# Waits for GpSimd behind VectorE's turn at the shared port, and a two-instruction conversion step planned as two

## The chip, the cores and the metric

One core of a Trainium2 chip runs the whole program. The metric is the device time of one execution in microseconds (us), from the first to the last instruction with the launch around it; the times given are medians of repeated runs. The engines are named as in the profile: PE is TensorE, DVE is VectorE, ACT is ScalarE, POOL is GpSimd, SP is SyncE.

## What is computed

Three stages follow each other, all in float32 (cut from the reference):

```python
# 1: attention with random features, 4 x 8 heads, 576 tokens, 64 wide, 128 features
h = x @ omega.T - (x * x).sum(-1, keepdims=True) / 2;  phi = exp(h - h.max(-1)) / sqrt(m)
num = q_p @ (k_p.T @ v);  x = num / (q_p @ k_p.sum(2) + 1e-6)
# 2: Fourier mixing over tokens and channels, layer norm, then 512 -> 2048 -> 512
u = x + real(fft(fft(x, axis=1), axis=2))
x = u + relu(norm(u) @ w_ch1) @ w_ch2
# 3: low-rank mixing over tokens, then a second 512 -> 2048 -> 512
u = x + (x.transpose(0, 2, 1) @ U @ V).transpose(0, 2, 1)
x = u + relu(u @ w_ch1) @ w_ch2
```

## The kernel before, in words

Every product that needs float32 accuracy is made from halves: a high part (written by ACT as a copy) and a low part (the value minus the high part, by DVE or POOL), three matmuls in place of one. 128 partitions by 384 columns is the usual tile of the two big layers. Most of these layers run in a scheme that forms sums and differences of hidden tiles and of weight tiles, so that 7 products serve for 8; these sums are DVE and POOL work as well. The attention and Fourier stages take the first 270 us or so, the two layers the rest, with the low-rank mixing around 620 to 710 us.

The weights of the two big layers come as 64-bit numbers, two 32-bit words each, from which a float32 tile is put together on the chip: 64 tiles of 128 x 512. `conv` (L881) plans one tile as: an SP load, two ACT copies (`a1`), then `a2`, which is two DVE `TENSOR_SCALAR` instructions on the same tile (L874 clamps, L876 shifts and masks; the second reads what the first wrote), then `conv_c` on DVE (L286, both operands in SBUF), then `conv_d` on POOL (L290, an integer add).

The order is not written by hand. `add` (L106) notes each step with the engines that may take it, a planned duration for each, and what it reads and writes. `plan` (L127) then places the steps one by one in a model of the engines, each at the engine that comes free first, those with the least slack first, and picks the engine of a step that may go to two. Steps marked `lock` are those whose DVE or POOL instruction takes the SBUF port that the two engines share: in the model (`held`) such a step on one of them waits until the other's has ended. `emit` (L241) issues the steps in the order of their planned starts. On the chip each engine takes its own instructions in that order, as soon as the data they read and the buffers they write allow it; nothing in the program made before tells POOL to wait for its planned turn at the port.

Of the kernel before, what the change touches and what calls it, by code (L numbers as in the profile page):

```python
# [12 lines left out]
U32 = mybir.dt.uint32  # L13
AF = mybir.ActivationFunctionType
ALU = mybir.AluOpType
# [20 lines left out]
F64_LO = 2.0**-15 * (1 + 0x100000 / 2**23)  # L36
# [55 lines left out]


class Op:
    __slots__ = ("eng", "fn", "lock", "main", "preds", "succs", "lst", "start", "end", "on", "left", "early", "soft", "raw")


class Sched:
    def __init__(self):
        self.on = False  # L100
        self.soft = True
        self.ops = []
        self.writer = {}
        self.readers = {}

    def add(self, eng, fn, r=(), w=(), lock=False, main=False, early=0.0):  # L106
# [5 lines left out]
        o.preds, o.succs, o.raw = set(), [], set()  # L112
        i = len(self.ops)
        for k in r:
            if k in self.writer:
                o.preds.add(self.writer[k])
                o.raw.add(self.writer[k])
            self.readers.setdefault(k, []).append(i)
        for k in w:
            if k in self.writer:  # L120
                o.preds.add(self.writer[k])
                o.raw.add(self.writer[k])
            o.preds.update(self.readers.get(k, ()))
            self.writer[k] = i
            self.readers[k] = []
        o.preds.discard(i)
        self.ops.append(o)  # L127

    def plan(self):
        ops = self.ops  # L130
        for i, o in enumerate(ops):
            for p in o.preds:
                ops[p].succs.append(i)
            o.left, o.on, o.lst = len(o.preds), None, None
# [12 lines left out]
        chain = [i for i, o in enumerate(ops) if o.main]  # L147
        pos, late = 0, 0.0
        nominal = sorted((o.lst, i) for i, o in enumerate(ops) if o.main or o.soft)
        at_ = 0  # L150
        free = dict.fromkeys(ENGS, 0.0)
        cand = {e: [] for e in ENGS}
        held = {"V": 0.0, "G": 0.0}

        def known(i):
            for e in ops[i].eng:
                cand[e].append(i)

        for i, o in enumerate(ops):
            if not o.left:  # L160
                known(i)
        at = {}

        def avail(i, e):
            if (i, e) not in at:
                at[(i, e)] = max([ops[p].end + ((SELF[e] if p in ops[i].raw else 0.0) if ops[p].on == e else LAT[ops[p].on]) for p in ops[i].preds], default=0.0)
# [12 lines left out]
        n, order = len(ops), []  # L179
        while len(order) < n:  # L180
            best = None
            for e in ENGS:
                for i in cand[e]:
                    o = ops[i]
                    if o.main and i != chain[pos]:
                        continue
                    v = max(free[e], avail(i, e))
                    if best is None or v < best[0] - 1e-9:
                        best = (v, e)
            t, e = best  # L190
            now, soon = [], []
            for i in cand[e]:
                o = ops[i]
                if o.main and i != chain[pos]:
                    continue
                v = avail(i, e)
                (now if v <= t + 1e-9 else soon).append((o.lst, i, v))
            l, i, v = min(now)
            o = ops[i]
            if len(o.eng) > 1 and later(i, e, t, late):  # L200
                alt = [x for x in now if len(ops[x[1]].eng) == 1 or not later(x[1], e, t, late)]
                if alt:
                    l, i, v = min(alt)
                    o = ops[i]
                else:
                    free[e] = max([t] + [free[x] for x in o.eng if x != e]) + 0.05
                    continue
            if e == "G" and any(x != i and ops[x].lock and ops[x].lst < l and ops[x].lst + late < t + o.eng["G"] and max([ops[p].end + LAT[ops[p].on] for p in ops[x].preds], default=0.0) < t + 0.3 for x in cand["V"]):
                free["G"] = max(t, free["V"]) + 0.05
                continue  # L210
            d = o.eng[e]
            w = [x for x in soon if x[2] < t + d and x[0] < t + d and x[0] < l]
            if w:
                m = min(x[2] for x in w)
                if l > m + d:
                    free[e] = m
                    continue
            o.start, o.end, o.on = t, t + d, e
            free[e] = t + d
            if o.lock and e in held:  # L220
                held[e] = t + d
            order.append(i)
            if o.main:
                pos += 1
            if o.main or o.soft:
                while at_ < len(nominal) and ops[nominal[at_][1]].on is not None:
# [12 lines left out]
        return order  # L239

    def emit(self):  # L241
        for i in self.plan():
            self.ops[i].fn(self.ops[i].on)


@with_exitstack
def tile_favor_fnet_moe(ctx: ExitStack, tc: tile.TileContext, qT, kT, v1, om, w1a, w2a, uu, vv, w1b, w2b, cs, cd, out):
# [35 lines left out]

    def conv_c(dst, high, s):
        mu = dst.bitcast(U32)
        nc.vector.scalar_tensor_tensor(out=mu, in0=high, scalar=0xC0000000, in1=mu, op0=ALU.bitwise_and, op1=ALU.bitwise_or)  # L286

    def conv_d(dst, high, s, aeng):
        mu = dst.bitcast(U32)
        aeng.tensor_tensor(out=mu, in0=mu, in1=s, op=ALU.add)  # L290

    def conv_b(dst, high, s, aeng=nc.vector):
        conv_c(dst, high, s)
# [58 lines left out]
        return (nxt_[k] - 1) % n  # L352

    def tt(e, o, x, y, op):
        ENG[e].tensor_tensor(out=o, in0=x, in1=y, op=op)  # L355

    def act(o, x, fn=AF.Copy):
        nc.scalar.activation(o, x, fn)  # L358
# [1 line left out]
    def cp(e, o, x):  # L360
        if e == "A":
            act(o, x)
        else:
            ENG[e].tensor_copy(out=o, in_=x)
# [497 lines left out]
    def sk(j):  # L862
        return ("wl", j) if j in (4, 5) else ("w", j - 6 if j in (6, 7) else j % 4 if j // 4 % 2 == 0 else 4 + j % 4)

    def conv(j, ex=()):
# [5 lines left out]

        def a2(e):
            d = box["c"][0]
            nc.vector.tensor_scalar(out=d, in0=d, scalar1=F64_LO, scalar2=F64_HI, op0=ALU.max, op1=ALU.min)  # L874
            mu = d.bitcast(U32)
            nc.vector.tensor_scalar(out=mu, in0=mu, scalar1=3, scalar2=0x3FFFFFF8, op0=ALU.logical_shift_left, op1=ALU.bitwise_and)  # L876
# [642 lines left out]
    def whole():  # L1519
# [109 lines left out]
        lnu_rs(2)  # L1629
        sch.soft = False  # L1630
        loop()
        sch.emit()

    E = mybir.EngineType
    with tc.manual_schedule(engines={E.PE, E.Activation, E.DVE, E.Pool, E.SP}):
# [86 lines left out]
```

## Time and profile before

| | |
|---|---|
| median of 3 runs | 1057.51 us (1056.8 to 1059.26) |
| the profiled execution, its own time | 1059.15 us |
| its span, first to last instruction | 1057.4 us |
| busy: PE, DVE, ACT, POOL | 1022.6, 918.0, 517.1, 434.5 us |
| mean granted clock of PE | 0.981 |

A busy time is the union of an engine's instructions; the rest of the span the engine was idle. What lies around the span (launch, end) is 1059.15 - 1057.4 = 1.75 us.

### The profile page before, as it was taken

The page shows a single profiled execution, that of the slowest core. Times are in us where ns is not written, and L with a number is a line of the kernel's source. Part 1 is how long each engine was busy: PE and PEld are TensorE (multiplying, and loading weights), DVE is VectorE, ACT ScalarE, POOL GpSimd, SP SyncE. Part 2 cuts the span into 40 slices and gives each one's busy share as a digit, 9 for nine tenths or more (in the row PEclk, how much of TensorE's full clock was granted, in tenths as well). Part 3 has the DMA queues.
Part 4 walks back from the last instruction along what each step waited for, and adds up shares of the span by engine and source line. Part 5 has one row for each costly group of instructions (what it writes and reads, how often), then busy time and mean ns, then how long its engine had stood idle before and what let it go on. Part 6 is the DMA issues. An engine that isn't in the chain of part 4 may idle for free.

```text
span 1057.4 us, 17131 instructions
## 1 busy us (share of the span) xinstructions
PE 1022.6 (97%) x6240; PEld 993.6 (94%) x6240; DVE 918.0 (87%) x1886; ACT 517.1 (49%) x1200; POOL 434.5 (41%) x429
## 2 busy tenths in 40 slices
PE   9999998889999999999999998999999999999998
PEld 8988998789899999999999997789999999999998
DVE  5788988697889999989999889989999999987766
ACT  6796767534455433434443456544544443533232
POOL 2275676243323341415442362623554353543211
PEclk9999999789999999999999998989999999999999
DMA  6544320010112200111210102002111111100013
GB/s 189 165 156 130 102 71 1 1 36 26 41 61 80 60 27 10 29 30 51 61 41 20 41 1 81 20 21 61 41 61 40 60 41 61 41 20 1 1 61 119
DMA packets 49091, 57.01 MB, mean 54 GB/s; under 512 B 3120, under 2 KB 42160, under 8 KB 48880
## 3 DMA queue, kind: packets, MB, share of 16 engines
q1 hardware_dynamic: 48720, 53.23, 16.7%
q0 software_dynamic: 288, 2.70, 0.7%
q8 instruction: 49, 0.80, 0.3%
q14 instruction: 34, 0.28, 0.1%
HBM read 51.20 MB, written 4.72 MB: 53 GB/s over the span
## 4 chain that ended last, share of the span: by engine, by line
PE 78%; DVE 14%; ACT 4%; POOL 2%; issue 1%; DMA 0%; SPq 0%; DVEq 0%; ACTq 0%; POOLq 0%
PE ph L964 10%; PE ph L965 10%; PE ph L966 10%; PE p L1225 9%; PE p L1223 9%; PE p L1224 8%; DVE uT L355 3%; PE pj L367 3%; PE kvp L367 3%; PE phu L964 1%; PE phu L965 1%; PE phu L966 1%; PE pn L367 1%; DVE hl L355 1%; PE acc L1000 1%
## 5 line engine op out<-in xcount | busy, mean ns | idle before, releaser
L355 DVE TENSOR_TENSOR uT<-uT,p 128x384 f32<-128x384 f32 x588 | 307.3, 548 | 48.7 <-PE p L1225 47.1
L290 POOL TENSOR_TENSOR w<-w,sc 128x512 uint32<-128x512 uint32 x64 | 95.9, 1502 | 138.8 <-DVE w L286 110.0
L964 PE MATMUL ph<-yh,ah 128*128 128x384 f32 x384 | 130.5, 340 | 0.6 <-ACT yh L358 0.6
L965 PE MATMUL ph<-yl,ah 128*128 128x384 f32 x384 | 130.3, 339 | 0.0
L966 PE MATMUL ph<-yh,al 128*128 128x384 f32 x384 | 130.3, 339 | 0.0
L1225 PE MATMUL p<-hl,bh_s 128*128 128x384 f32 x294 | 100.2, 341 | 3.3 <-DVE hl L355 3.2
L1223 PE MATMUL p<-hh,bh_s 128*128 128x384 f32 x294 | 99.6, 339 | 0.7 <-ACT hh L358 0.7
L1224 PE MATMUL p<-hh,bl_s 128*128 128x384 f32 x294 | 98.7, 336 | 0.0
L964 PE MATMUL ph<-xh,ah 128*128 128x384 f32 x288 | 97.1, 337 | 0.0
L966 PE MATMUL ph<-xh,al 128*128 128x384 f32 x288 | 96.9, 336 | 0.0
L965 PE MATMUL ph<-xl,ah 128*128 128x384 f32 x288 | 96.8, 336 | 0.0
L482 ACT ACTIVATE phi<-pj,mx 128x128 f32<-128x128 f32 x288 | 82.3, 382 | 19.0 <-DVE mx L469 18.8
L355 POOL TENSOR_TENSOR hl<-r,hh 128x384 fp32r<-128x384 f32 x37 | 41.1, 1110 | 108.6 <-ACT hh L358 101.8
L358 ACT ACTIVATE r<-ph 128x384 f32<-128x384 f32 x66 | 32.4, 491 | 102.4 <-PE ph L966 102.3
L358 ACT ACTIVATE hh<-t 128x384 fp32r<-128x384 f32 x72 | 37.9, 527 | 86.4 <-DVE t L949 83.0
L964 PEld LDWEIGHTS ph<-yh,ah 128*128 128x128 f32 x384 | 73.2, 191 | 1.5 <-ACT yh L358 0.8
L965 PEld LDWEIGHTS ph<-yl,ah 128*128 128x128 f32 x384 | 73.0, 190 | 0.7 <-DVE yl L355 0.4
L358 ACT ACTIVATE hh<-f 128x384 fp32r<-128x384 f32 x60 | 31.6, 526 | 85.5 <-DVE f L355 32.2
L966 PEld LDWEIGHTS ph<-yh,al 128*128 128x128 f32 x384 | 73.0, 190 | 0.0
L1223 PE MATMUL p<-hh,bh_a 128*128 128x384 f32 x210 | 71.7, 341 | 0.1
L1225 PE MATMUL p<-hl,bh_a 128*128 128x384 f32 x210 | 71.3, 340 | 0.0
L1224 PE MATMUL p<-hh,bl_a 128*128 128x384 f32 x210 | 71.1, 338 | 0.0
(736 smaller groups left out, 2963.5 us busy)
## 6 DMA issues: line engine op xcount, KB each, us to landing
raw<-in_w1a_dram SPq DMA_DIRECT2D x16, 512.0 KB, 3.8
raw<-in_w2a_dram SPq DMA_DIRECT2D x16, 512.0 KB, 3.7
raw<-in_w2b_dram SPq DMA_DIRECT2D x16, 512.0 KB, 3.6
raw<-in_w1b_dram SPq DMA_DIRECT2D x16, 512.0 KB, 3.8
raw<-in_qT_dram SPq DMA_DIRECT2D x18, 256.0 KB, 3.1
out_dram<-uT SPq DMA_DIRECT2D x24, 192.0 KB, 2.0
raw<-in_kT_dram SPq DMA_DIRECT2D x17, 256.0 KB, 3.2
vt<-in_v_dram SPq DMA_DIRECT2D x16, 260.0 KB, 2.8
```

The lines of the kernel that those rows point to most:

```text
L290: aeng.tensor_tensor(out=mu, in0=mu, in1=s, op=ALU.add)
L355: ENG[e].tensor_tensor(out=o, in0=x, in1=y, op=op)
L358: nc.scalar.activation(o, x, fn)
L367: nc.tensor.matmul(o, w, m, start=start, stop=stop, skip_group_check=True)
L482: nc.scalar.activation(phi_[n][:, h, :], pj_[(n, g)][:, h - 4 * g, :], AF.Exp, bias=mx_[n][:, h : h + 1])
L964: nc.tensor.matmul(ph, wh[:, c], xh[:, r, :], start=(r == 0), stop=False)
L965: nc.tensor.matmul(ph, wh[:, c], xl[:, r, :], start=False, stop=False)
L966: nc.tensor.matmul(ph, wl[:, c], xh[:, r, :], start=False, stop=(r == 3))
L1000: nc.tensor.matmul(a, wh[:, c], hh, start=(f == 0), stop=False)
L1223: nc.tensor.matmul(a, wh[:, cc], hh, start=first, stop=False, skip_group_check=True)
L1224: nc.tensor.matmul(a, wl[:, cc], hh, start=False, stop=False, skip_group_check=True)
L1225: nc.tensor.matmul(a, wh[:, cc], hl, start=False, stop=True, skip_group_check=True)
```

## The change

`conv` plans the two `TENSOR_SCALAR` instructions as two steps, `a2` and `a3`, of 0.4 us each in the planner's numbers, where one step of 0.8 us held both. In `plan`, a POOL step that takes the port is looked at once more when it is placed: `v` is the time at which its own inputs and the POOL step before it would let it start, and `past` the DVE port steps that end after that and no later than its planned start. If there is such a step, apart from one that had simply begun first, POOL's instruction gets a wait (`after`) for the last of them, and its planned start moves behind that DVE step's end by the latency in `LAT`. `emit` hands the wait to the framework as a dependency between the two instructions. Everything that follows is planned with the moved times, so engines and places of other steps change too.

```diff
+        last = {"V": 0.0, "G": 0.0}
+        locked = []
...
             d = o.eng[e]
+            hold = None
+            if e == "G" and o.lock:
+                v = max([last["G"]] + [ops[p].end + (SELF["G"] if ops[p].on == "G" else LAT[ops[p].on]) for p in o.preds])
+                past = [x for x in locked[-40:] if ops[x].end > v and ops[x].end <= t + 1e-6]
+                if past and (len(past) > 1 or ops[past[0]].start > v or t > ops[past[0]].end + 0.1):
+                    hold = past[-1]
...
+            if hold is not None:
+                o.after = hold
+                t = max(t, ops[hold].end + LAT["V"])
             o.start, o.end, o.on = t, t + d, e
...
             if o.lock and e in held:
                 held[e] = t + d
+                if e == "V":
+                    locked.append(i)
+            if e in last:
+                last[e] = t + d
...
-    def emit(self):
+    def emit(self, dep):
         for i in self.plan():
-            self.ops[i].fn(self.ops[i].on)
+            o = self.ops[i]
+            self.ins = None
+            o.fn(o.on)
+            o.ins = self.ins
+            if o.after is not None:
+                dep(o.ins, self.ops[o.after].ins)
...
+    def dep(x, y):
+        tc.add_manual_dep(x, y.name, mybir.DependencyInfo(mybir.DependencyClass.Sync, mybir.DependencyReason.SCHED_ONLY), reason="port")
...
-        add({"V": 0.8}, a2, ex, [sk(j)], lock=True)
+        add({"V": 0.4}, a2, ex, [sk(j)], lock=True)
+        add({"V": 0.4}, a3, ex, [sk(j)], lock=True)
```

The new field `slack` is 0 everywhere. In the changed program 44 POOL instructions carry a wait for a DVE instruction that they did not have, or for a later one than they had. Of 5161 steps 129 change engine: 61 from POOL to DVE, 51 from DVE to POOL, 9 from DVE to ACT, 7 from ACT to DVE, 1 from ACT to POOL. DVE gets 8 instructions more, POOL 9 fewer.

POOL's instructions where the Fourier stage's folds begin, some 62 us into the execution; `z0o` is a sum or difference of folded tokens, `e20o` an intermediate, and the brackets name the engines that an instruction waits for. Before:

```order
34 L355 TENSOR_TENSOR z0o_940<-e20o_880 128x128 [waits Pool_49]
35 L355 TENSOR_TENSOR z0o_940<-e20o_880 128x128
36 L355 TENSOR_TENSOR z0o_980<-eo_1o 128x256 [waits Pool_49]
37 L355 TENSOR_TENSOR z0o_980<-e20o_971 128x128 [waits DVE_49]
38 L355 TENSOR_TENSOR e20e_1022<-eo_1e 128x256 [waits DVE_49,Pool_49]
```

And in the changed program:

```order
34 L376 TENSOR_TENSOR z0o_940<-e20o_880 128x128 [waits DVE_49,Pool_49]
35 L376 TENSOR_TENSOR z0o_940<-e20o_880 128x128
36 L376 TENSOR_TENSOR e20o_971<-eo_1o 128x256 [waits Pool_49]
37 L376 TENSOR_TENSOR z0o_992<-eo_1o 128x256
38 L376 TENSOR_TENSOR zl0o_942<-z0o_940,zh0o_941 128x512 [waits DVE_49,Activation_49]
```

The first `z0o` now waits for a DVE instruction as well, the intermediate `e20o_971` has come over from DVE, and the low part `zl0o_942` has too, with a wait of its own.

DVE's instructions some 80 us into the execution; `x` is a tile of attention output made from `den` and its reciprocal, `abl` a low part that PE waits for, and `w` are weight tiles in conversion. Before:

```order
125 L355 TENSOR_TENSOR abl_0_1220<-ps_0e,abh_0_1219 128x2x146
126 L549 TENSOR_SCALAR den_0_1232<-pn_0_1212 128x4
127 L874 TENSOR_SCALAR w_1205<-w_1205 128x512
128 L876 TENSOR_SCALAR w_1205<-w_1205 128x512
129 L565 RECIPROCAL den_0_1232<-den_0_1232 128x4
130 L355 TENSOR_TENSOR abl_0_1220<-ps_0o,abh_0_1219 128x2x144
131 L549 TENSOR_SCALAR den_1_1256<-pn_1_1234 128x4
132 L554 TENSOR_TENSOR x_1231<-pn_0_1212,den_0_1232 128x256
133 L565 RECIPROCAL den_1_1256<-den_1_1256 128x4
134 L286 SCALAR_TENSOR_TENSOR w_1205<-raw_1142,w_1205 128x512
135 L554 TENSOR_TENSOR x_1231<-pn_1_1234,den_1_1256 128x256
136 L286 SCALAR_TENSOR_TENSOR w_1131<-raw_966,w_1131 128x512
```

And in the changed program, where the same tile of attention output is `x_1209`:

```order
123 L573 TENSOR_SCALAR den_0_1210<-pn_0_1155 128x4
124 L573 TENSOR_SCALAR den_1_1215<-pn_1_1174 128x4
125 L589 RECIPROCAL den_0_1210<-den_0_1210 128x4
126 L589 RECIPROCAL den_1_1215<-den_1_1215 128x4
127 L578 TENSOR_TENSOR x_1209<-pn_0_1155,den_0_1210 128x256
128 L376 TENSOR_TENSOR abl_0_1213<-ps_0e,abh_0_1212 128x2x146
129 L578 TENSOR_TENSOR x_1209<-pn_1_1174,den_1_1215 128x256
130 L898 TENSOR_SCALAR w_1065<-w_1065 128x512
131 L388 COPY qpT_1255<-pt_0_1234 128x512
132 L902 TENSOR_SCALAR w_1065<-w_1065 128x512
133 L898 TENSOR_SCALAR w_1239<-w_1239 128x512
134 L307 SCALAR_TENSOR_TENSOR w_1065<-raw_966,w_1065 128x512
```

Both halves of `x` now stand ahead of the conversions that they stood between, and the two `TENSOR_SCALAR` of a tile (L898 and L902) have another instruction between them. Of the 64 pairs 57 are apart in the changed program.

## Rows read from the trace of the kernel before

**Rows 1.** Windows by stage: length, busy us (instructions) of PE, PEld, DVE, ACT, POOL, clock, DMA.
```profile
0.00:300.00 300.00, 280.48 (x2057) 270.24 (x2057) 239.34 (x541) 187.77 (x525) 142.99 (x152) 0.96 0.28 83
300.00:600.00 300.00, 298.23 (x1706) 296.07 (x1705) 281.56 (x570) 125.01 (x259) 106.67 (x98) 1.00 0.14 42
600.00:710.00 110.00, 102.51 (x544) 89.89 (x544) 98.49 (x189) 61.77 (x125) 51.33 (x51) 0.94 0.10 29
710.00:1057.40 347.40, 341.43 (x1940) 337.37 (x1938) 298.60 (x589) 142.51 (x291) 133.53 (x128) 1.00 0.15 47
```

**Rows 2.** Timeline, first and last stretched DVE instruction: start us, us, engine, line, instruction.
```profile
13.69 0.71 DVE L364 CAST th<-raw 128x512 fp32r<-128x512 f32 x1
...
957.33 0.92 DVE L355 TENSOR_TENSOR w<-w,st 128x256 f32<-128x256 f32 x1
```

**Rows 3.** Lines 876 and 874, tile eo_1e: ns min/median/max, first and last start.
```profile
L876 DVE TENSOR_SCALAR w<-w x64: 426/428/1408, 72.2 to 942.1; 128x512 uint32<-128x512 uint32 x64
L874 DVE TENSOR_SCALAR w<-w x64: 407/420/1521, 71.8 to 941.6; 128x512 f32<-128x512 f32 x64
L355 DVE TENSOR_TENSOR eo_1e<-x,x x3: 674/685/927, 64.1 to 217.4; 128x512 f32<-128x512 f32 x3
```

**Rows 4.** Timeline at 62 to 68 us; brackets: idle before, and who ended it.
```profile
62.73 0.69 DVE L355 TENSOR_TENSOR z0o<-eo_0o 128x256 f32<-128x256 f32 x1
...
64.08 0.93 DVE L355 TENSOR_TENSOR eo_1e<-x,x 128x512 f32<-128x512 f32 x1
64.93 0.41 DVE L355 TENSOR_TENSOR e20o<-eo_1o 128x256 f32<-128x256 f32 x1
...
67.17 0.99 PE L367 MATMUL pn<-kv,qpT 128*128 128x65 f32 x7 [1.13 <-ACT qpT L358]
```

**Rows 5.** Timeline at 78 to 86 us.
```profile
78.09 1.39 DVE L876 TENSOR_SCALAR w<-w 128x512 uint32<-128x512 uint32 x1
...
83.19 1.71 DVE L286 SCALAR_TENSOR_TENSOR w<-raw,w 128x512 uint32<-128x512 uint32 x1
83.23 0.54 PE L702 MATMUL pdp0r<-abh,cdt 128*128 128x290 f32 x2 [0.90 <-ACT qpT L358]
...
84.98 1.27 POOL L290 TENSOR_TENSOR w<-w,sc 128x512 uint32<-128x512 uint32 x1 [0.63 <-DVE w L286]
85.94 0.61 PE L664 MATMUL ps_1e<-cst,zh0e 128*128 128x292 f32 x1 [1.58 <-ACT uT L358]
```

**Rows 6.** Timeline at 263 to 267 us, the third block's layer norm.
```profile
263.92 1.43 POOL L290 TENSOR_TENSOR w<-w,sc 128x512 uint32<-128x512 uint32 x1 [4.41 <-DVE w L286]
264.26 1.52 DVE L355 TENSOR_TENSOR c_2True<-uT,mean 128x384 f32<-128x384 f32 x1
...
265.70 0.55 DVE L355 TENSOR_TENSOR xl<-c_1True,xh 128x384 fp32r<-128x384 f32 x1
266.30 0.45 PE L965 MATMUL phu<-xl,ah 128*128 128x384 f32 x1 [1.23 <-DVE xl L355]
```

**Rows 7.** Timeline at 513 and at 665 us, the big layers.
```profile
513.86 0.44 PE L1225 MATMUL p<-hl,bh_s 128*128 128x384 f32 x1 [0.64 <-DVE hl L355]
...
665.15 1.23 DVE L355 TENSOR_TENSOR hl<-t,hh 128x384 fp32r<-128x384 f32 x1
...
666.44 0.45 PE L1225 MATMUL p<-hl,bh_s 128*128 128x384 f32 x1 [0.66 <-DVE hl L355]
```

**Rows 8.** Timeline at 219 to 228 us: POOL's longest instruction, and a wait of PE.
```profile
219.99 6.66 POOL L290 TENSOR_TENSOR w<-w,sc 128x512 uint32<-128x512 uint32 x1 [3.30 <-ACT zh3o L358]
...
227.15 1.22 PE L849 MATMUL prs<-ident,rc 128*128 128x128 f32 x4 [3.85 <-ACT qs2r L358]
```

**Rows 9.** Windows at 85, 220 and 223 us, columns as in Rows 1.
```profile
85.00:90.00 5.00, 4.05 (x20) 4.06 (x21) 3.57 (x7) 3.87 (x13) 5.00 (x5) 0.66 0.84 245
219.99:226.65 6.66, 3.31 (x21) 2.80 (x19) 6.66 (x19) 0.76 (x2) 6.66 (x2) 0.93 0.26 79
223.00:233.00 10.00, 6.15 (x21) 5.15 (x20) 9.70 (x24) 2.43 (x5) 4.89 (x3) 0.66 0.01 2
```

More of the change, by code (lines that the diff above doesn't have):

```diff
@@ L94 @@
 class Op:
-    __slots__ = ("eng", "fn", "lock", "main", "preds", "succs", "lst", "start", "end", "on", "left", "early", "soft", "raw")
+    __slots__ = ("eng", "fn", "lock", "main", "preds", "succs", "lst", "start", "end", "on", "left", "early", "soft", "raw", "after", "ins", "slack")
 class Sched:
@@ L104, in __init__, with add @@
         self.readers = {}
-    def add(self, eng, fn, r=(), w=(), lock=False, main=False, early=0.0):
+        self.ins = None
+    def add(self, eng, fn, r=(), w=(), lock=False, main=False, early=0.0, slack=0.0):
         if not self.on:
@@ L111, in add @@
         o.eng, o.fn, o.lock, o.main, o.early, o.soft = eng, fn, lock, main, early, self.soft and "P" in eng
-        o.preds, o.succs, o.raw = set(), [], set()
+        o.preds, o.succs, o.raw, o.slack = set(), [], set(), slack
         i = len(self.ops)
@@ L133, in plan @@
                 ops[p].succs.append(i)
-            o.left, o.on, o.lst = len(o.preds), None, None
+            o.left, o.on, o.lst, o.after = len(o.preds), None, None, None
         t = 0.0
@@ L165, in avail @@
             if (i, e) not in at:
-                at[(i, e)] = max([ops[p].end + ((SELF[e] if p in ops[i].raw else 0.0) if ops[p].on == e else LAT[ops[p].on]) for p in ops[i].preds], default=0.0)
+                at[(i, e)] = max([ops[p].end + ((SELF[e] if p in ops[i].raw else 0.0) if ops[p].on == e else LAT[ops[p].on]) for p in ops[i].preds], default=0.0) + ops[i].slack
             v = at[(i, e)]
@@ L239, in plan @@
         return order
-    def emit(self):
+    def emit(self, dep):
         for i in self.plan():
-            self.ops[i].fn(self.ops[i].on)
+            o = self.ops[i]
+            self.ins = None
+            o.fn(o.on)
+            o.ins = self.ins
+            if o.after is not None:
+                dep(o.ins, self.ops[o.after].ins)
 @with_exitstack
@@ L285, in conv_c @@
         mu = dst.bitcast(U32)
-        nc.vector.scalar_tensor_tensor(out=mu, in0=high, scalar=0xC0000000, in1=mu, op0=ALU.bitwise_and, op1=ALU.bitwise_or)
+        sch.ins = nc.vector.scalar_tensor_tensor(out=mu, in0=high, scalar=0xC0000000, in1=mu, op0=ALU.bitwise_and, op1=ALU.bitwise_or).ins
     def conv_d(dst, high, s, aeng):
         mu = dst.bitcast(U32)
-        aeng.tensor_tensor(out=mu, in0=mu, in1=s, op=ALU.add)
+        sch.ins = aeng.tensor_tensor(out=mu, in0=mu, in1=s, op=ALU.add).ins
     def conv_b(dst, high, s, aeng=nc.vector):
@@ L354, in tt @@
     def tt(e, o, x, y, op):
-        ENG[e].tensor_tensor(out=o, in0=x, in1=y, op=op)
+        sch.ins = ENG[e].tensor_tensor(out=o, in0=x, in1=y, op=op).ins
+    def dep(x, y):
+        tc.add_manual_dep(x, y.name, mybir.DependencyInfo(mybir.DependencyClass.Sync, mybir.DependencyReason.SCHED_ONLY), reason="port")
     def act(o, x, fn=AF.Copy):
@@ L363, in cp @@
         else:
-            ENG[e].tensor_copy(out=o, in_=x)
+            sch.ins = ENG[e].tensor_copy(out=o, in_=x).ins
     def mm(o, w, m, start, stop):
@@ L873, in a2, with a3 @@
             d = box["c"][0]
-            nc.vector.tensor_scalar(out=d, in0=d, scalar1=F64_LO, scalar2=F64_HI, op0=ALU.max, op1=ALU.min)
-            mu = d.bitcast(U32)
-            nc.vector.tensor_scalar(out=mu, in0=mu, scalar1=3, scalar2=0x3FFFFFF8, op0=ALU.logical_shift_left, op1=ALU.bitwise_and)
+            sch.ins = nc.vector.tensor_scalar(out=d, in0=d, scalar1=F64_LO, scalar2=F64_HI, op0=ALU.max, op1=ALU.min).ins
+        def a3(e):
+            mu = box["c"][0].bitcast(U32)
+            sch.ins = nc.vector.tensor_scalar(out=mu, in0=mu, scalar1=3, scalar2=0x3FFFFFF8, op0=ALU.logical_shift_left, op1=ALU.bitwise_and).ins
         add({"S": S512}, lambda e: w_load(j), [], [("raw", j % 2)])
         add({"A": 1.1}, a1, [("raw", j % 2)] + ex, [sk(j), ("s", j % 2)])
-        add({"V": 0.8}, a2, ex, [sk(j)], lock=True)
+        add({"V": 0.4}, a2, ex, [sk(j)], lock=True)
+        add({"V": 0.4}, a3, ex, [sk(j)], lock=True)
         add({"V": V512}, lambda e: conv_c(*box["c"]), [("raw", j % 2)] + ex, [sk(j)], lock=True)
@@ L1631, in whole @@
         loop()
-        sch.emit()
+        sch.emit(dep)
     E = mybir.EngineType
```

## The prediction

> **What bounds the kernel now.** I read the windows by stage first [rows 1]. TensorE is the engine with least idle time: 19.5 us (300 - 280.48) in the first 300 us, 1.8 us from 300 to 600, 7.5 us from 600 to 710 and 6.0 us in the last 347, together 34.8 of the 1057.4 us span. A gain can only come out of these 34.8 us, or out of stretches in which TensorE runs at a lower clock. VectorE is second, 281.56 of 300 us from 300 to 600: it has little room there, but TensorE idles only 1.8 us in that stage, so VectorE's lateness is mostly absorbed by work that lies ahead in buffers.
>
> Then I looked in the timeline for VectorE instructions that took longer than others of the same shape. 97 of them are over 0.1 us longer and have a GpSimd instruction running across them; the first is a cast at 13.69 us, the last at 957.33 us [rows 2]. Their excess adds up to 60.3 us. By the order in which the program issues its steps, GpSimd's instruction belongs behind VectorE's in 65 of the 97 (47.0 us): GpSimd's data were there early and it took the port before its turn. The clearest group is L876: the median is 428 ns and the longest 1408, with 13 of the 64 stretched [rows 3]. It reads what L874 wrote just before, and in the pause between the two GpSimd comes in.
>
> 47 us of stretched VectorE work is not 47 us of the span. So the third view is TensorE's idle gaps, each followed back to what was late. The ones over 0.25 us that have a stretched VectorE instruction in their chain are five places:
>
> - 67 us: TensorE idles 1.13 us behind an ACT copy that follows VectorE's work; ahead of it are a difference of folds at 62.73 (0.69 us where the same shape takes 0.41 at 64.93) and an `eo` at 64.08 (0.93 us, median 0.685) [rows 3, 4].
> - 83 and 86 us: gaps of 0.90 and 1.58 us, with L876 at 1.39 and the conversion's L286 at 1.71 us ahead of them [rows 5].
> - 266 us: 1.23 us, behind `c_2True`, 1.52 us under a GpSimd `conv_d` (L290), where the same size takes 0.55 [rows 6].
> - 513.86 us: 0.64 us, behind a `hl` that is late [rows 7].
> - 666 us: 0.66 us, behind a `hl` of 1.23 us [rows 7].
>
> Together the gaps are 6.14 us (1.13 + 0.90 + 1.58 + 1.23 + 0.64 + 0.66). The other idle time comes from elsewhere: the start, ACT and matmul chains, and one gap of 3.85 us at 227 us of the opposite kind [rows 8], below.
>
> **What the change adds and moves.** Instruction work hardly changes: the split of the conversion step adds nothing, since the two instructions existed, and eight more on VectorE for nine fewer on GpSimd are 8 x 0.4 to 0.7 us, 3 to 6 us over 1057, on an engine that idles 139 us (1057.4 - 918.0). The 44 waits cost no instruction of their own; each delays a GpSimd instruction to the end of a VectorE one. What is queued behind it on GpSimd (low parts of weights and of `h`, the next `conv_d`, its two DMA issues) is delayed with it. SP's loads are issued in almost the same order.
>
> The waits are where GpSimd was planned to be late. Of the 65 out-of-turn cases only 15, with 9.4 us of the 47.0, get a wait that directly holds the offender behind the instruction that it stretched. 16 (13.2 us) have the GpSimd instruction planned ahead now or between the two halves of the conversion, 17 (14.4 us) have no wait, and in the rest one of the two has gone to another place or engine. So I don't expect the 47 us to vanish; perhaps half does, and new encounters arise. I therefore price the five places alone, by what stands there in the changed order.
>
> *67 us.* The excess of the fold (0.69 - 0.41 = 0.28) and of `eo` (0.93 - 0.685 = 0.25) is taken away by the wait, and `e20o` (0.41 us) leaves VectorE for GpSimd [rows 3, 4]: 0.94 of the 1.13 us. Bounds: 0 and 1.13. **-0.94**
>
> *83 and 86 us.* Both halves of `x` come ahead of the conversions, so neither a stretched L876 nor L286 stands before them. But a copy of `x` goes from ACT to GpSimd, behind a held `conv_d`, and what waits for it arrives later. Bounds: 0 and 2.48; I take half. **-1.24**
>
> *266 us.* `c_2True` is now several places ahead of the instruction for which the `conv_d` waits, so it can't be stretched: 1.52 - 0.55 = 0.97 of the 1.23 us [rows 6]. **-0.97**
>
> *513 and 666 us.* At 513 half of the 0.64 us; at 666 the excess is 1.23 - 0.55 = 0.68, all of the gap, but another low part now stands before it on GpSimd: 0.4. Bounds: 0 and 1.30 [rows 6, 7]. **-0.7**
>
> *227 us.* Here the late one is GpSimd: its `conv_d` begins at 219.99 and takes 6.66 us, as long as the window in which VectorE is busy for 6.66 us with 19 instructions, one after the other [rows 8, 9]. ACT and TensorE wait for what follows it (3.85 us), and TensorE's clock falls: the mean granted clock is 0.66 from 223 to 233 us. In the changed order the same `conv_d` waits for an instruction near the end of that row and is let go 0.1 to 0.2 us later than it won the port before. The stall stays. **+0.2**
>
> *New encounters.* A block at full size costs what the longest of L874 does over its median, 1.52 - 0.42 = 1.10 us [rows 3]. With 129 steps on other engines I count one that lands where TensorE has nothing ahead; bounds 0 (all covered) and four of them, 4.4 us. **+1.1**
>
> The sum is -0.94 - 1.24 - 0.97 - 0.7 + 0.2 + 1.1 = -2.55 us. The profiled execution would be 1059.15 - 2.55 = 1056.6; it lies 1.64 us above the median of the runs, so the median would be 1057.51 - 2.55 = **1055.0 us**.
>
> **A rule against the change.** The row at 83.19 shows a release: L286 ends at 84.90, GpSimd's `conv_d` starts at 84.98 [rows 5]. The row at 219.99 shows that a waiting GpSimd does not simply get the next turn, as 19 VectorE instructions went by [rows 8, 9].
> The Trainium skill, page "SBUF — State Buffer", section "SBUF: two separate sides", says that the pair is an exclusive lock: whoever starts first holds it for the whole instruction and the other is fully blocked. The stretched rows agree with that. By it a held GpSimd instruction that comes after one VectorE instruction blocks the next one in its place, so the blocks would only move and the sum would be nothing.
>
> **Rivals.**
> *The blocks move on (no change).* A wait that ends with one VectorE instruction lets GpSimd in at the following one, which is then stretched by the same 1.0 us. For it: 33 of the out-of-turn cases get no wait at the place or are planned in front. Against it: at the five places the next instruction is often not one on which TensorE waits. The gains of 3.85 us are cut to about 1 and the new encounters take that: 1057.5 us.
>
> *GpSimd starves behind its wait (slower).* The wait's signal comes some 0.08 us after VectorE's end, and by then VectorE has started the next instruction; in a full row of VectorE work GpSimd then loses again and again, as at 219.99 us. Place: the Fourier stage to 270 us and the stretch from 450 to 600, where 7 more instructions (some 3.9 us) come to VectorE. Price: another stall such as at 227 us, 3.85 us, and the lower clock after it, 10 us at 0.66, which loses up to 3.4 us; less the gains, about +5: 1062 us. It decides as soon as one `conv_d` takes over 4 us and is followed by a TensorE gap.
>
> *The gains are larger.* All of the 6.14 us go, with no new encounter, and the dip of the clock behind the gap at 86 us (0.66 from 85 to 90 us, 1.7 us lost [rows 9]) goes too: 1057.5 - 6.1 - 1.7 = 1049.7 us.
>
> **How the numbers follow.** Chances: small gain as in the sum 0.45 (1052.5 to 1057.5); larger gain 0.15 (1049 to 1052.5); no change 0.18 (1056 to 1059); slower 0.22 (1059.5 to 1064). 0.2% is 2.1 us, about what a measurement of this kernel can tell from no change: below 1055.4 is faster, above 1059.6 slower. The small gain's centre is near the border, so a little over half of it counts as faster: 0.25 + 0.15 = 0.40. Same: 0.20 and most of the no change, 0.15: 0.35. Slower: 0.22, and 0.03 of the no change whose new encounters weigh more. The range of 1050.0 to 1061.5 leaves out the best end of the larger gain and the far part of the slower case; the likeliest case by itself has 1052.5 to 1057.5.
>
> **What would show it.** In the changed kernel's profile, the stretched L876 (there L902) should be fewer than 13 and its mean near the median; the gaps of TensorE at 67 and 266 us should be below 0.3 us; the gaps at 83 and 86 us about half; the `conv_d` near 220 us still above 6 us with its gap behind it. TensorE's idle time should be 32 us or so in place of 34.8. Wrong on the slow side: GpSimd instructions of over 4 us in more places, and TensorE idle behind low parts made by GpSimd. Wrong on the fast side: TensorE idle under 30 us and the dips at 85 or 227 us gone.

## The result, and the profile after

The changed kernel takes 1041.51 us (median, 1040.94 to 1043.4); the kernel before took 1057.95 us beside it. The ratio is 0.9847, 95% interval 0.983 to 0.9865: 16.4 us faster. I had forecast 1055.0 us with a range from 1050.0, so the direction was right and the size far too small. The profiled execution took 1040.94 us, its span is 1039.1 us against 1057.4, 18.3 us less, at a mean granted clock of 0.986 against 0.981. The profiled execution of the kernel before lies 1.2 us above its median and that of the changed kernel 0.6 below, so about 2 of the 18.3 us are the choice of executions.

The windows by stage of the changed kernel, columns as in [rows 1]:

```profile
0.00:300.00 300.00, 282.16 (x2105) 273.61 (x2106) 234.92 (x551) 191.23 (x532) 132.92 (x156) 0.98 0.27 84
300.00:600.00 300.00, 300.00 (x1725) 298.47 (x1724) 274.54 (x576) 130.16 (x270) 108.94 (x103) 1.00 0.14 43
600.00:710.00 110.00, 104.38 (x558) 94.00 (x556) 96.26 (x197) 60.21 (x121) 50.16 (x52) 0.94 0.11 34
710.00:1039.10 329.10, 324.72 (x1858) 323.62 (x1856) 276.77 (x571) 136.53 (x280) 113.98 (x111) 1.00 0.15 46
```

TensorE idles 27.8 us (1039.1 - 1011.3) in place of 34.8. That is only 7.0 of the 18.3 us. The other 11.3 us came out of what the page calls TensorE's busy time, 1022.6 before and 1011.3 now, for the same 6240 matmuls. The row from 300 to 600 shows how to read this: 1725 matmuls in 300 us where 1706 stood before.

The views of the two halves of the conversion in the changed kernel, to be held against [rows 3]:

```profile
L902 DVE TENSOR_SCALAR w<-w x64: 399/421/429, 72.8 to 926.9; 128x512 uint32<-128x512 uint32 x64
L898 DVE TENSOR_SCALAR w<-w x64: 408/422/971, 72.1 to 923.7; 128x512 f32<-128x512 f32 x64
```

No second half is stretched any more (429 ns at most, 1408 before). Read as for the prediction, the stretched VectorE instructions with a GpSimd instruction across them are 43 with 19.1 us, before 97 with 60.3. Out of turn are 5 with 1.1 us, before 65 with 47.0; those that the plan itself puts behind GpSimd rose from 32 (13.3 us) to 38 (18.0 us).

Where the 18.3 us lie shows when the start of each matmul is compared with that of the same matmul before. Differences by stage, in the time of the kernel before (us; the two traces' starts subtracted, the labels are those of the experiments below). Each row is one execution: those of e1, e4 and e7 lie 3.1, 2.4 and 2.3 us above the medians of their kernels, and the first 60 us differ by up to 1.6 us between kernels of the same order (changed kernel, e2, e5, e6).

```
                     0-60  60-120 120-300 300-600 600-720 720-end
changed kernel       -0.1   -4.7    -3.6    -2.9    -3.7    -3.3
e1 waits only        +1.1   +0.1    -1.9    -2.9    -3.6    -2.6
e2 order only        +0.7   -1.3    +2.0    -0.2    -0.5    -2.3
e3 split only         0.0   +1.1     0.0    -0.5    -3.8    -2.4
e5 early waits        0.0   -4.7    -3.5    -0.4    +0.5    -2.3
e6 late waits        +1.5   -1.3    +1.9    -2.9    -1.9    -3.3
e7 split and waits    0.0   -0.1    -2.1    -2.9    -5.5    -3.3
e12 four early       +1.0   -1.8    +4.7    -0.5    -1.7    -2.2
```

9.9 us came from 300 us on, where I had counted 0.7.

### The profile page after: what moved, and what is told of

Same layout as the page of the kernel before. It is cut to its first block, busy times and chain, and to the rows that moved or that the text cites. A ratio compares the mean times of both kernels' runs of the same rounds, so it can differ in the third digit from the quotient of the medians.

```text
span 1039.1 us, 17145 instructions
## 1 busy us (share of the span) xinstructions
PE 1011.3 (97%) x6240; PEld 989.7 (95%) x6240; DVE 882.5 (85%) x1894; ACT 518.1 (50%) x1201; POOL 406.0 (39%) x420
## 3 DMA queue, kind: packets, MB, share of 16 engines
q1 hardware_dynamic: 48720, 53.23, 16.7%
## 4 chain that ended last, share of the span: by engine, by line
PE 91%; DVE 5%; ACT 2%; POOL 1%; issue 1%; DMA 0%; SPq 0%; DVEq 0%; ACTq 0%; POOLq 0%
PE ph L991 11%; PE ph L992 11%; PE ph L993 11%; PE p L1250 10%; PE p L1252 10%; PE p L1251 10%; PE pj L391 4%; PE kvp L391 3%; PE pn L391 2%; PE phu L991 2%; PE phu L992 2%; PE phu L993 1%; PE acc L1027 1%; PE acc L1029 1%; PE acc L1028 1%; PE pt L544 1%
## 5 line engine op out<-in xcount | busy, mean ns | idle before, releaser
L311 POOL TENSOR_TENSOR w<-w,sc 128x512 uint32<-128x512 uint32 x64 | 89.1, 1394 | 175.9 <-DVE w L307 119.3
L382 ACT ACTIVATE hh<-f 128x384 fp32r<-128x384 f32 x60 | 31.6, 527 | 81.4 <-DVE f L376 27.6
```

The source lines that it names most:

```text
L311: sch.ins = aeng.tensor_tensor(out=mu, in0=mu, in1=s, op=ALU.add).ins
```

## The experiments

Theory W: the waits alone keep GpSimd to its turn, and that is the gain. Its rivals: O, the moved order and engines (or the split) make it; M, the blocks move on to the next VectorE instruction; and later a throttle theory, that any wait which thins out GpSimd's starts helps. Medians and ratios stand beside the kernel before on the same chip; "out of turn" is counted as above.

**e1, waits only.** From the changed kernel, the conversion step left as one and no start moved, which gives the order of before:

```diff
-                t = max(t, ops[hold].end + LAT["V"])
...
-        add({"V": 0.4}, a2, ex, [sk(j)], lock=True)
-        add({"V": 0.4}, a3, ex, [sk(j)], lock=True)
+        add({"V": 0.8}, a2, ex, [sk(j)], lock=True)
```

> The order and engines of the kernel before, with 53 waits put on GpSimd instructions by the same rule, no planned start moved and the conversion step left as one. In the trace of before these waits would stand behind 52 of the 65 out-of-turn cases (37.5 of 47.0 us). Theory W (the waits alone keep GpSimd to its turn and that is the gain): stretched VectorE time falls from 60 us to about 23 us; the change took it from 60.3 to 19.1 us for a gain of some 16 us, so 0.4 us per us, and this kernel comes to 1041 to 1046 us. Theory O (the gain is that of the moved order and engines): 1054 to 1060 us. Theory M (a held GpSimd instruction blocks the next VectorE instruction instead): stretched time stays above 45 us and the time stays at 1056 to 1060 us.

1046.41 us, ratio 0.9883 (0.9864 to 0.9902): 11 us of the 16, with order and engines of before. Out of turn 16 with 11.6 us; all stretched time together is some 29 us, more than the 23 expected and far less than M's 45. O alone and M fall. What is left is mostly the second half of the conversion, which no wait guards here. Its view in e1:

```profile
L899 DVE TENSOR_SCALAR w<-w x64: 426/427/1409, 73.0 to 932.4; 128x512 uint32<-128x512 uint32 x64
```

12 of the 64 are still stretched, 13 before.

**e2, order only.** The changed kernel without the dependency:

```diff
-            if o.after is not None:
-                dep(o.ins, self.ops[o.after].ins)
```

> The order, engines and split of the changed kernel, without the 44 waits. Theory W: out-of-turn cases come back, 40 us or more of stretched VectorE time, 1052 to 1060 us. Theory O: 1041 to 1046 us, with few out-of-turn cases. Theory M: as the changed kernel, 1040 to 1044 us, since the waits do nothing.

1058.3 us, ratio 1.0005 (0.9995 to 1.0015), as W had it: out of turn 47 with 30.0 us, all stretched time together some 43 us, and nothing gained. The windows from 300 to 600 us of e1, then of e2:

```profile
300.00:600.00 300.00, 300.00 (x1725) 299.09 (x1723) 274.70 (x575) 127.26 (x263) 104.70 (x100) 1.00 0.14 43
```

```profile
300.00:600.00 300.00, 299.03 (x1707) 296.10 (x1707) 275.07 (x571) 125.07 (x261) 109.05 (x99) 1.00 0.15 43
```

The order of before with waits has the 1725 matmuls of the changed kernel; the order of the changed kernel without waits has 1707, as before.

**e3, split only.** Both edits: the dependency left out as in e2, and the start not moved as in e1.

> The conversion step planned as two instructions and nothing else: no waits, no start moved for them. Theory W: 1053 to 1060 us, out-of-turn cases as before. Theory O in its form that the split lets the planner place work between the two halves: 1043 to 1050 us, with the stretched L876 gone.

1054.14 us, ratio 0.9969 (0.9958 to 0.9981), in W's bounds, but the split has 3.4 us of its own. The second half is stretched once instead of 13 times, since the planner now sets something between the halves and the pause in which GpSimd came in is filled (56 of the 64 pairs have another VectorE instruction between them). Out of turn 41 with 26.3 us.

**e4, no split.** The changed kernel with the conversion step as one (the second edit of e1).

> The waits and the moved planned starts, with the conversion step left as one (62 waits). Theory W: 1041 to 1048 us, and what is left over the changed kernel is the stretched second half of the conversion, 13 cases of some 1 us before, of which the waits don't hold those planned right at its end. Theory O in its split form: 1052 to 1060 us.

1044.28 us, ratio 0.987 (0.9849 to 0.989), as W had it; out of turn 13 with 9.4 us, of which 8 second halves with 7.2 us.

**e5 and e6, waits of one part.** The changed kernel, with this condition, and with its opposite:

```diff
-            if o.after is not None:
+            if o.after is not None and self.ops[o.after].end < 265.0:
```

> The changed kernel with only the 23 of its 44 waits that stand before the planned time 265 us, up to the third block of the Fourier stage; same order. Theory W with the stages independent: the first 300 us as in the changed kernel (8.3 us less than before in the comparison of TensorE's starts), the rest as in the order without waits (3.1 us less): 1046 us (1044 to 1048). If the gain of the early waits is given back later: 1050 us or more.

> The changed kernel with only the 21 later waits; same order. Theory W with the stages independent: the first 300 us as in the order without waits (1.3 us more than before), the rest as in the changed kernel (9.9 us less): 1048 to 1051 us. If the waits of the big layers did nothing, because TensorE has hidden tiles ahead there: 1055 us or more.

1049.41 us, ratio 0.9929 (0.9915 to 0.9942), and 1053.0 us, ratio 0.9962 (0.995 to 0.9975). Both parts gain, and the first 300 us of e5 are those of the changed kernel in the table. But both came out slower than expected, e5 by 1.4 us over its bound and e6 by 2. Against e2, with the ratios, since the runs were on different chips, the two gain 0.76% and 0.43%, some 8.0 and 4.5 us, together 1.19% and 12.6 us; all waits gain 1.58%, 16.7 us. The table puts most of the missing part into 600 to 720 us (e5 and e6 less e2 make -0.9 there, the changed kernel has -3.7), where an order without waits is worth anything from -3.8 (e3) to -0.5 (e2). The granted clock dips to 0.5 there in every one of these runs, for 3.4, 6.8 or 10.2 us at a time; what sets their length stays open.

**e7, split and waits.** The changed kernel without the moved start (the first edit of e1).

> The order of the split alone (e3) with 43 waits by the same rule, no planned start moved. Theory W: the waits are worth 9 us or more on any order: 1041 to 1046 us against 1054 without them. Theory that the planned starts have to move with the waits, or the wait comes in the way of the next VectorE step: 1049 us or more.

1043.38 us, ratio 0.9873 (0.9857 to 0.9889); out of turn 1 with 0.3 us. W holds on a third order: by the ratios some 10 us less than e3, which is this kernel without waits. The moved starts add what the table shows from 60 to 300 us, but by the ratios the changed kernel is only 0.26% below e7, and the intervals overlap.

**e8 and e12, the wrong turn.** The same order, each wait on the VectorE port instruction planned one place, or four places, ahead:

```diff
-                o.after = hold
+                o.after = locked[locked.index(hold) - 1] if locked.index(hold) else None
```

> The changed kernel's order with its 44 waits, each on the VectorE port instruction planned just before the one of the changed kernel. GpSimd then gets loose one turn too soon. Theory W (what counts is whose turn it is): the instruction that was guarded is stretched again, 30 us or more of stretched VectorE time, 1050 to 1058 us. Theory of the throttle (any wait that thins out GpSimd's starts helps, whichever instruction it names): 1041 to 1046 us.

> The changed kernel's order with each wait on the VectorE port instruction four places ahead of the one that the changed kernel names; e8 with one place ahead kept the whole gain. Theory W, with the turn as what counts: GpSimd comes loose some 2 us early, out-of-turn cases come back to 15 us or more, 1048 to 1058 us. Throttle theory (any wait that thins out GpSimd's starts): 1041 to 1044 us.

One place: 1042.27 us, ratio 0.9861 (0.9848 to 0.9874), the whole gain kept, with 14 cases of 6.6 us out of turn. W's forecast for it, 1050 us or more, failed, and the throttle theory's 1041 to 1046 came out. Four places: 1058.55 us, ratio 1.0007 (0.9995 to 1.0019), the whole gain lost, out of turn 48 with 31.6 us. That is W's forecast but for 0.55 us, yet it does not fell the throttle theory, because little of a throttle was left: four places ahead, only 16 of the 44 waits ask for more than the instruction's own data do, and 9 of these 16 instructions start within 0.3 us of the end of the one named. One place ahead these are 41 and 35. So which instruction has to be named is not shown to within one place. What the runs do show is that the gain goes with the time out of turn: 30.0 us in e2, 31.6 in e12 and 26.3 in e3 at 1058.3, 1058.55 and 1054.14 us; 11.6 in e1 and 9.4 in e4 at 1046.41 and 1044.28; 6.6 in e8, 1.1 in the changed kernel and 0.3 in e7 at 1042.27, 1041.51 and 1043.38.

The timelines show why one place ahead is not yet too soon. First the kernel before, then the changed kernel, then e8, around the same `conv_d`:

```profile
507.08 0.69 DVE L286 SCALAR_TENSOR_TENSOR w<-raw,w 128x512 uint32<-128x512 uint32 x1
...
507.75 0.56 DVE L355 TENSOR_TENSOR hl<-f,hh 128x384 fp32r<-128x384 f32 x1
507.85 1.61 POOL L290 TENSOR_TENSOR w<-w,sc 128x512 uint32<-128x512 uint32 x1 [0.69 <-DVE w L286]
508.23 1.51 DVE L355 TENSOR_TENSOR b_s<-w,b_s 128x256 fp32r<-128x256 f32 x1
```

```profile
497.84 0.56 DVE L376 TENSOR_TENSOR hl<-f,hh 128x384 fp32r<-128x384 f32 x1 [0.24 <-ACT hh L382]
498.32 0.42 DVE L898 TENSOR_SCALAR w<-w 128x512 f32<-128x512 f32 x1
498.81 1.29 POOL L311 TENSOR_TENSOR w<-w,sc 128x512 uint32<-128x512 uint32 x1 [1.57 <-DVE w L898]
499.31 0.56 DVE L376 TENSOR_TENSOR uT<-uT,p 128x384 f32<-128x384 f32 x1 [0.57 <-PE p L1252]
499.78 0.55 DVE L976 SCALAR_TENSOR_TENSOR hl<-ph,hh 128x384 fp32r<-128x384 f32 x1
```

```profile
498.27 0.56 DVE L376 TENSOR_TENSOR hl<-f,hh 128x384 fp32r<-128x384 f32 x1 [0.24 <-ACT hh L382]
498.75 0.42 DVE L898 TENSOR_SCALAR w<-w 128x512 f32<-128x512 f32 x1
498.91 1.40 POOL L311 TENSOR_TENSOR w<-w,sc 128x512 uint32<-128x512 uint32 x1 [1.23 <-DVE hl L376]
499.74 0.55 DVE L376 TENSOR_TENSOR uT<-uT,p 128x384 f32<-128x384 f32 x1 [0.57 <-PE p L1252]
```

Before, `conv_d` starts as soon as its data are there, behind L286, and the low part `b_s` behind it takes 1.51 us where 0.42 is usual. In the changed kernel it waits for L898, starts 0.08 us after that has ended (498.32 + 0.42 = 498.74, 498.81), and beside it run instructions that read PSUM (`p`, `ph`), at 0.56 and 0.55 us, unstretched. In e8 it waits for the `hl` one place ahead, but is let go at 498.91, when L898 has run since 498.75: L898 keeps its 0.42 us and `conv_d` takes 1.40 us, 0.11 more. VectorE has here started its next instruction before GpSimd is let go, and so it has for 30 of the 44 held instructions of the changed kernel. A wait that names one place too early can then still come out right: by name the waits of e8 guard 24 of the 47 cases of e2, and 33 fewer are left. 14 did not come out right.

**e9 and e10, the stall at 217 us.** The copy `qs` of the Fourier stage shares a tile with the conversion, the `s` that `conv_d` reads. e9 is the changed kernel with

```diff
-            box["qs"] = cv.tile([128, 512], F32, tag=f"s{si}", name=f"qs{b}{nm}")[:, 0:NEO]
+            box["qs"] = cv.tile([128, NEO], F32, tag="q0", name=f"qs{b}{nm}")
```

and e10 has besides, as e13 below, no moved start late in the plan:

```diff
-                t = max(t, ops[hold].end + LAT["V"])
+                if t < 265.0:
+                    t = max(t, ops[hold].end + LAT["V"])
```

> The changed kernel, same order and waits; the Fourier stage's copy qs has a buffer of its own, where it shared one with the conversion (the tile s that conv_d reads). Theory B (the 4.06 us gap of TensorE at 217 us is the copy qs2r waiting until the late conv_d lets go of the shared buffer): the copy comes some 4 us earlier, TensorE then waits for the reciprocal alone, and 1.5 to 2.5 us go, 1039 to 1041 us, with up to 3.4 us more if the dip of the clock behind it goes. Theory V (VectorE has too much to do there, and the copy's wait is only beside it): the gap stays within 0.5 us of 4.06, 1041 to 1043 us.

> As e9, and beyond the planned time 265 us the waits are given without moving the planned starts (46 waits, 15 steps on other engines, all after 300 us). e7, which moved none, was 1.7 us quicker from 600 to 720 us than the changed kernel. If the order there did that: 1.5 to 2 us under e9, 1036 to 1039 us. If it was the chance of one dip of the clock: as e9.

1044.02 us, ratio 0.9876 (0.9855 to 0.9898), and 1044.5 us, ratio 0.9875 (0.9856 to 0.9894): neither gains on the changed kernel, both lie 2.5 to 3 us above it. Neither theory had this. e14 and e15 show where the loss comes from.

**e13, late starts unmoved.** The second edit of e10 alone.

> The changed kernel with shared buffers as they were; beyond the planned time 265 us the waits are given without moving the planned starts (46 waits, 15 steps on other engines, all after 300 us). If the order made that way is what made e7 quicker from 600 to 720 us: 1039 to 1041 us, with TensorE's matmul step from 720 us on at 174.5 ns as in the changed kernel. If it was the chance of the clock's dips: 1041 to 1043 us.

1040.67 us, ratio 0.9851 (0.9835 to 0.9866). The median lies in the first bounds, but the ratio cannot be told from the changed kernel's 0.9847. No order gain can be claimed from it; e7's 600 to 720 us was likely one shorter dip of the clock, 3.4 us at 692 us where the changed kernel has 6.8.

**e14 and e15, the size of a buffer.** e14 is e9 with `[128, 384]` for `[128, NEO]` (NEO is 290). e15 is the changed kernel with an unused tile in its place:

```diff
     cv = ctx.enter_context(tc.tile_pool(name="cv", bufs=1))
+    pad = cv.tile([128, NEO], F32, tag="q0", name="pad")
+    nc.gpsimd.memset(pad[:, 0:1], 0.0)
```

> As e9, with the own buffer 384 numbers wide (1536 bytes a partition) in place of 290 (1160 bytes). In e9 and e10 alone the matmul step from 720 us on was 175.1 ns, in the twelve other profiles 174.5. Theory A (what lies behind the odd-sized buffer is moved to other addresses, and that costs the step): 174.5 ns again and 1040.5 to 1042 us. Theory Q (the earlier copy itself does it): 175.1 ns and 1043.5 to 1045 us. The gap at 217 us is as in e9 in both, 2.5 us and 0.9 us behind it.

> The changed kernel with an unused buffer of 290 numbers (1160 bytes) in the same place, one element of it set at the start; qs keeps its shared buffer. Theory A: the matmul step from 720 us on is 175.1 ns, and the kernel takes 1043 to 1045 us. Theory Q: 174.5 ns and 1041 to 1043 us.

e14: 1042.29 us, ratio 0.986 (0.9844 to 0.9876). e15: 1045.05 us, ratio 0.9886 (0.9871 to 0.9901). The matmul steps, 174.5 and 175.15 ns, are those of theory A; the times lie 0.3 and 0.05 us above its bounds. The windows from 750 to 1000 us of the changed kernel, e9, e14 and e15, in this order:

```profile
750.00:1000.00 250.00, 250.00 (x1434) 250.00 (x1433) 215.07 (x445) 106.46 (x218) 88.89 (x87) 1.00 0.11 35
```

```profile
750.00:1000.00 250.00, 250.00 (x1430) 250.00 (x1430) 214.55 (x444) 106.55 (x219) 89.41 (x87) 1.00 0.11 35
```

```profile
750.00:1000.00 250.00, 250.00 (x1434) 250.00 (x1433) 215.19 (x445) 106.99 (x219) 90.00 (x87) 1.00 0.11 35
```

```profile
750.00:1000.00 250.00, 250.00 (x1430) 250.00 (x1429) 214.46 (x445) 106.50 (x218) 88.32 (x86) 1.00 0.11 35
```

With the odd buffer, used or not, 1430 matmuls pass in 250 us, without it 1434, and TensorE shows no idle time in any of them. And e14, free of that, shows what the copy's wait was worth. In the changed kernel the copy starts right behind `conv_d`:

```profile
218.79 1.26 POOL L311 TENSOR_TENSOR w<-w,sc 128x512 uint32<-128x512 uint32 x1 [8.79 <-DVE rc L882]
...
220.09 0.41 ACT L382 ACTIVATE qs2r<-pdq2r 128x290 f32<-128x290 f32 x1 [4.47 <-POOL w L311]
```

And in e14:

```profile
216.92 0.41 ACT L382 ACTIVATE qs2r<-pdq2r 128x290 f32<-128x290 f32 x1
...
220.19 1.26 POOL L311 TENSOR_TENSOR w<-w,sc 128x512 uint32<-128x512 uint32 x1 [8.79 <-DVE rc L882]
220.35 1.62 PE L873 MATMUL prs<-ident,rc 128*128 128x128 f32 x6 [2.46 <-DVE rc L882]
...
222.88 1.65 PE L805 MATMUL pmn<-s,ones 128*128 128x384 f32 x2 [0.92 <-DVE pmm2r L376]
```

The copy now comes long before `conv_d`; TensorE waits 2.46 us for VectorE's reciprocal and then 0.92 us for VectorE again, 3.38 us in place of 4.06, and no time is gained that the runs can tell. Theory B's 1.5 to 2.5 us did not go. Theory V is nearer, though 0.68 is a little over its 0.5: what TensorE waits for there is VectorE's row of folds and layer norm.

**e11, a wait in every case.**

```diff
-                if past and (len(past) > 1 or ops[past[0]].start > v or t > ops[past[0]].end + 0.1):
+                if past:
```

> The changed rule without its exception: a GpSimd port step waits for the last VectorE port step that ends between its own readiness and its planned start, in every case (148 waits in place of 44; 142 steps on other engines than in the changed kernel). Theory W: the out-of-turn cases that are left in the changed kernel (5, 1.1 us) are too few to matter, 1040 to 1043 us. If each wait costs something of itself (the signal takes 0.08 to 0.15 us behind the VectorE instruction's end, on an engine that is not the bound): still 1040 to 1044. If the moved plan matters: planned work ends later, 1045 us or more.

1049.2 us, ratio 0.9918 (0.9901 to 0.9934). Nothing is out of turn any more, but the plan of these 148 waits has 24.1 us of VectorE time behind GpSimd, against 18.0, and the layer around 600 to 720 us costs 1.6 us more than before where the changed kernel saves 3.7. So keeping every turn is not enough. Which part of the loss the waits make and which the 142 steps on other engines, this run does not separate. No version beats the changed kernel by what the runs can tell.

## Why the prediction was wrong

**The five places.** The step of the sum that failed is "I therefore price the five places alone". By the starts of the matmuls behind the gaps they came to -0.58 us (67 us), -2.5 (83 and 86), -0.96 (266), -0.77 (513) and -0.82 (666), together -5.6, where I had -3.85; a new gap at 74 us took 0.6 back, where I had 1.1. Only at 513 and 666 us does that pass a bound, 1.59 for 1.30. The other 13 or so of the 18.3 us lie outside the five places, where I had no gain: 9.9 us came from 300 us on, and only 1.6 of them at 513 and 666. The prediction's own sign of being wrong on the fast side, TensorE idle under 30 us and the dip at 85 us gone, came true.

Gaps of TensorE in the changed kernel, in its timeline:

```profile
66.45 1.11 PE L391 MATMUL pn<-kv,qpT 128*128 128x65 f32 x8 [0.55 <-ACT qpT L382]
...
74.23 1.08 PE L391 MATMUL pn<-kv,qpT 128*128 128x65 f32 x8 [0.95 <-DVE x L578]
...
220.56 0.79 PE L873 MATMUL prs<-ident,rc 128*128 128x128 f32 x2 [4.06 <-ACT qs2r L382]
...
258.01 0.45 PE L992 MATMUL phu<-xl,ah 128*128 128x384 f32 x1 [0.27 <-DVE xl L376]
```

At 67 us [rows 4] 1.13 became 0.55, -0.58 where I had -0.94. At 266 us [rows 6] 1.23 became 0.27: -0.96, where I had -0.97. At 513 us I had -0.3, at 666 us -0.4; no gap is left at either. From 60 to 120 us the starts give -4.7, where I had -0.94 and -1.24: the gaps at 83 and 86 us [rows 5] are gone but for 0.44, and the dip of the clock behind them [rows 9] with them. That dip was in my rival of larger gains; it belonged in the sum.

**What the list left out.** It said that no other gap over 0.25 us has a stretched VectorE instruction in its chain. But the kernel before has this one, with the first half of a conversion stretched from 0.42 to 0.98 us ahead of it:

```profile
644.59 0.98 DVE L874 TENSOR_SCALAR w<-w 128x512 f32<-128x512 f32 x1
...
646.46 0.97 PE L1454 MATMUL pu<-vh,mxl 96*128 96x288 f32 x2 [1.33 <-DVE uT L355]
```

The start behind it moved by -1.15 us. Three more gaps, of 0.68 us at 386.47, 0.70 at 669.15 and 0.69 at 827.13, end a wait for VectorE or for what follows it and are gone as well, -0.84, -0.86 and -0.85 us; how far back VectorE's lateness there goes was not traced.

**What the idle time hides.** "A gain can only come out of these 34.8 us" or the lower clock was wrong too, and so was the sentence that VectorE's lateness from 300 us on "is mostly absorbed". TensorE's idle time is less than its loss. Rows of the kernel before, TensorE at 385 us:

```profile
385.28 0.34 PE L965 MATMUL ph<-xl,ah 128*128 128x384 f32 x1
385.45 0.34 PE L966 MATMUL ph<-xh,al 128*128 128x384 f32 x1
386.47 0.44 PE L1223 MATMUL p<-hh,bh_s 128*128 128x384 f32 x1 [0.68 <-ACT hh L358]
```

Each matmul is shown as 0.34 us, but the next begins 0.17 us after it. From 385.45 to 386.47 are 1.02 us, a loss of 0.85 where the page has 0.68 of idle; a halt of under 0.17 us shows none. Counted by starts, less the usual step of each shape (0.173 us for 128x384), TensorE lost 74.9 us before and loses 56.6 now. The difference of 18.3 us must be the span's, since the matmuls are the same; the two sums depend on the step taken. From 300 to 600 us it lost 6.3 (idle 1.8), now 3.3; with the median step, 0.174 us, 4.6 and 1.6.

So the 18.3 us are 7.0 of idle time, some 5 of the clock and some 6 that show as neither. The clock's part: 1057.4 x (1 - 0.981) = 20.1 us of full speed were withheld before, 1039.1 x (1 - 0.986) = 14.5 now. The dip behind 86 us is gone, one of 3.4 us at 185 us too, and the one of 10.2 us behind 192 us is now 6.8. The last is in part chance: in e14 and e15, with the same order, it is 10.2 us again.

**What the waits reach.** I counted 15 cases (9.4 us) as directly held and took half of 47 us to vanish, with new encounters at +1.1. 60 of the 65 went, and 45.9 of the 47.0 us. The moved order alone took less than half of that: in e2 47 cases with 30.0 us are left. Of these 47 the 44 waits hold 35 by a wait on the GpSimd instruction itself, and 7 more because GpSimd takes its instructions in order, so that a wait holds everything behind it as well. That leaves 5, as found. I had compared the waits with the cases in the old order, and so missed those that the new order makes and the waits then hold. In e1, the old order, the waits stand behind 52 of the 65 cases. And the new plan doesn't set GpSimd anew where it collides: of the 44 held instructions 43 start 0.08 to 0.26 us after the end of the named one, and only 7 have a stretched VectorE instruction beside them.

**The 227 us stall.** The size was right, +0.2 predicted and 4.06 for 3.85 us [rows 8], though a new gap of 1.65 us, a wait for VectorE, stands ahead of it at 214.49 us. The cause was half right. `conv_d` was late and held the copy through the shared tile, but most of TensorE's wait stays without it (e14). And I expected it above 6 us again: 5.4 of its 6.66 us were waiting, as the same instruction now takes 1.26 us (218.79 in the changed kernel, above) and the copy still follows right behind it. GpSimd's time beyond the usual of each shape fell from 31.8 to 13.8 us in all; no run separates what that is worth.

**The rivals.** *The blocks move on* fell with e1 and the seven of 44. In the changed kernel 660 VectorE instructions that read PSUM run beside GpSimd for over 0.1 us, and none is stretched; of 111 with two inputs from SBUF 33 are, and of 57 with one input, from SBUF, 10, all of them `TENSOR_SCALAR` or casts. So the block doesn't move on where the plan has a reader of PSUM next, as at 499.31 and 499.78, and I had overlooked that. The rule of the Trainium skill, page "SBUF — State Buffer", section "SBUF: two separate sides", brings a VectorE instruction into the lock by two SBUF inputs, if the GpSimd instruction reads SBUF, or by a mode that uses two ports; these counts agree with it, though the trace does not show in which mode an instruction ran. *GpSimd starves* did not happen: the longest GpSimd instruction of the changed kernel takes 1.80 us. *The gains are larger* was the right rival, and its gain, down to 1049.7 us, was still too small because it counted only the five gaps and one dip.

## What to carry to other kernels

For an engine whose instructions overlap, count instructions in a window and compare starts; idle time is here less than what it loses, and halts under 0.17 us don't show in it at all. A planner's order holds across two engines only if something enforces it: order and split alone (e2) were worth nothing here, 53 waits on the old order 11 us (e1), all together 16 us. A wait holds the whole queue behind it, so judge a set of waits by what it reaches in the new order, and let the held instruction loose where its neighbour on the other engine reads PSUM.

## What the runs showed that I had not expected

An unused buffer of 1160 bytes a partition made the kernel 3.5 us slower than the changed kernel (e15, 1045.05 against 1041.51), with the same instructions and order on VectorE: the mean step of the matmuls shorter than 0.2 us from 720 to 1030 us was 175.15 ns in the three kernels with it and 174.5 ns in the fourteen others, the one with a buffer of 1536 bytes among them. From 750 to 1000 us both kinds of matmul of the layer take longer: `ph<-yl,ah` 175.3 ns a step against 174.0, `p<-hh,bl_s` 175.0 against 174.0. In the built programs the tiles behind the buffer, `yh`, `yl`, `hh` and `hl` among them, lie 1184 bytes further on with it and 1536 with the larger one. That the size matters is shown; which address it is that costs, and why, was not tried.
